# Opening stage of a gated attention and GEGLU kernel: neighbouring banks for the first units' sum pairs, three banks for the second transposes, first weights in two parts

## The chip, the core and the metric

The kernel runs on one core of a Trainium2 chip. The metric is the device time of one execution in microseconds (us). A core has a matrix engine (PE in the profile, with its weight loads as PEld), a vector engine (DVE), a scalar engine (ACT), a GpSimd engine (POOL) and a sync engine (SP), which here only issues transfers. Each engine runs its own instructions strictly in order; semaphores order them across engines. Matrix products land in eight accumulator banks, which DVE and ACT read.

## What is computed

From `reference.py`, cut to what matters:

```python
qkv = x @ wqkv                                   # 32 heads of 32
logits over 8 keys per position, 2 apart; softmax; weighted sum; @ wo     -> a
b = (gelu(x @ w_gate) * (x @ w_up)) @ w_down
g = sigmoid((x * gate_w).sum(-1, keepdims=True))
return g * a + (1 - g) * b
```

There are 2048 tokens of 1024 features; the hidden width of the second branch is 3584. All tensors are bf16.

## The kernel before

The large products are done by Winograd's form of Strassen's method on 2x2 blocks: seven block products in place of eight, paid for with sums of blocks on DVE. Tokens are handled in two halves (`s` = 0, 1) of 1024, each in two chunks of 512 columns. `c1` and `c2` hold the transposed x of the two chunks of a half; their first four and last four slices of 128 features are the blocks R11, R21 and R12, R22. T1 to T4 are sums of these blocks.

A `Unit` makes 256 outputs of one weight (two times 128) for one half of the tokens. Its products are groups of four matmuls of 128x512, each group one method call:

- `p1_` (L325 and on): L11 by R11 into bank X; ACT then copies X to bank Y (L363).
- `p2`: L12 by R21 on top of X, then ACT empties X (L347 with GELU for a gate unit, L349 for others).
- `p5`: S1 by T1 into bank V, copied out by ACT (L368).
- `p6`: S2 by T2 on top of Y; ACT copies Y to bank Z (L376).
- `p73`: S3 by T3 on top of Y, S4 by R22 on top of Z; then one DVE instruction (L387) reads Z and Y as a pair and adds the product of `p5`. Its access pattern starts at Z and steps by the distance from Z to Y (`yz`).
- `p4`: L22 by T4 on top of Y, ACT empties Y (L347 or L349), and for a gate unit applies GELU to what L387 wrote (L395).

`lie(x, v, y, z)` says which of the banks 0 to 7 a unit uses as X, V, Y, Z. Waits are set by what an instruction reads or writes, and an access that steps from one bank to another is held against everything from its first to its last byte.

The opening stage, `head()`, writes its order out by hand. It has four units: f0 and f1 (gate and up of the first pair of weight columns), f2 and f3 (gate and up of the second pair). On PE it runs in this order:

1. six warm-up matmuls (L151), then the transposes of chunk 0 (L215), emptied by DVE (L221) and ACT (L219) in turn;
2. `p1_` of f0 and f1, one small transpose (`patterns`, L260), `p2` of f0 and f1, `p1_` of f2 and f3;
3. the transposes of chunk 1, `p2` of f2 and f3, and `gate_chunk` for both chunks (L270: the mixing gate g, emptied by ACT at L273 and stored by POOL at L275);
4. `p5` of f0 to f3, `p6` of f0 to f3, `p73` of f0 to f2, `p4` of f0 to f2.

DVE meanwhile makes T1 to T4 (L1239), the sums of the first weights (`sums_pair`, L311: four steps for each pair, s0 and s1) and part of the sums of the query and key weights (`sums_qk`, L447). After `head()`, a loop over the other units runs `p1` of a unit, `p73` of the one before, `p5`, `p2` and `p6`, and `p4` of the one before; its first unit has number 2 and uses X = 0, V = 1, Y = 2, Z = 3. f3's `p73` and `p4` fall into that first round. In the gaps a planner spends a time credit per unit on DVE's background work (sums of blocks, softmax, attention products), among it `x_forms(1)` (L200), the sums for the second half of the tokens, whose x comes transposed by DMA (L328).

All weight and x loads of the opening are issued in order by SP: x of chunk 0 (two of its four tiles by ACT), the first 128 columns of the four first weight pieces (L167), x of chunk 1 (L143), the second 128 columns of these four (L167), the query and key weights (L324), 16 transposing loads (L328). A transfer counts on one of eight semaphores, taken in turn; an issue waits until the transfer eight places ahead of it has landed.

The lines that the prediction goes through are these:

```python
units[0:Q0] = f[2:]
for u, x, v, y, z in zip(f, (0, 1, 3, 5), (3, 5, 0, 1), (2, 6, 7, 4), (0, 1, 3, 5)):
    u.lie(x, v, y, z)
...
pair = _win_ap(self.Z, [[self.yz * SC, 2], [1, SC]])
```

Of the kernel before, what the change touches and what calls it, by code (L numbers as in the profile page):

```python
# [10 lines left out]
BF16 = mybir.dt.bfloat16  # L11
# [4 lines left out]
P = 128  # L16
SC = 512
# [51 lines left out]
def kernel(  # L69
# [12 lines left out]
    nc = tc.nc  # L82
# [3 lines left out]
    x = A_x.rearrange("b s d -> (b s) d")  # L86
    o2 = out.rearrange("b s d -> (b s) d")
    KT = D // P
    HK = KT // 2
# [17 lines left out]
    def reg3(kb, a, b):  # L107
        return reg(kb, a * b).rearrange("p (a b) -> p a b", a=a)

    def reg4(kb, a, b, c):  # L110
        return reg(kb, a * b * c).rearrange("p (a b c) -> p a b c", a=a, b=b)

    def regf(kb, n):
        return reg(kb, 2 * n).bitcast(F32)
# [3 lines left out]
    def bank(i):  # L118
        return banks[:, i, :]
# [17 lines left out]
    with tc.manual_schedule(engines={mybir.EngineType.PE, mybir.EngineType.DVE, mybir.EngineType.Activation,  # L137
# [9 lines left out]
        warm = reg(R_ST, SC)  # L147
        V.memset(warm, 0.0)
        for i in range(NWARM):
            pw = bank((2, 4, 6, 7)[i % 4])  # L150
            nc.tensor.matmul(pw, lhsT=warm[:, 0:P], rhs=warm, start=True, stop=True)  # L151
        wj = consts.tile([P, 1], F32, name="wj")
        nc.scalar.activation(out=wj[:], in_=warm[:, 0:1], func=ACT.Gelu_apprx_tanh)
# [5 lines left out]
        raw0 = reg4(R_W0, 2, KT, 2 * P)  # L159
# [1 line left out]
        sums0, sums1 = (reg(o, 4 * 2 * HK * P).rearrange("p (f m k n) -> p f m k n", f=4, m=2, k=HK)  # L161
                        for o in (R_WQK + 48, R_W0 + 16))

        def load_pair(dst, i, a=0, b=2 * P):
            c0 = 2 * P * i
            for m, src in ((0, B_w_gate), (1, B_w_up)):
                nc.sync.dma_start(out=dst[:, m, :, a:b], in_=src[:, c0 + a:c0 + b].rearrange("(k p) n -> p k n", p=P))  # L167

        gwr = small.tile([KT, P], BF16, tag="gwr", bufs=1)
        nc.gpsimd.dma_start(out=gwr[:], in_=gate_w.rearrange("(k p) -> k p", p=P))  # L170
        load_pair(raw0, 0, 0, P)
        load_pair(raw1, 1, 0, P)
        load_xn(1)
        load_pair(raw0, 0, P, 2 * P)
# [6 lines left out]
        for s in range(2):  # L181
            b0 = R_X[s]
            f = XF()
# [10 lines left out]
        def flat(a):  # L194
            return a.rearrange("p a b -> p (a b)")
# [8 lines left out]
            f = xf[s]  # L204
            TT(out=flat(f.T3), in0=flat(f.R22), in1=flat(f.R12), op=ALU.subtract)

        def pe_transpose_chunk(c, dst, slots, by_k):
            order = [(j, k0) for j in range(4) for k0 in range(0, KT, 4)]
            if by_k:
                order.sort(key=lambda g: g[1])  # L210
            for n_, (j, k0) in enumerate(order):
                i, o = slots[n_ % 4]
                p_ = bank(i).bitcast(BF16)[:, o * SC:(o + 1) * SC].rearrange("p (a b) -> p a b", a=4)
                for kk in range(4):
                    nc.tensor.transpose(out=p_[:, kk, :], in_=xn[c % 2][:, j, (k0 + kk) * P:(k0 + kk + 1) * P],  # L215
                                        identity=ident[:])
                d = dst[:, k0:k0 + 4, j * P:(j + 1) * P]
                if n_ % 2 == 1:
                    nc.scalar.copy(out=d, in_=p_)  # L219
                else:  # L220
                    V.tensor_copy(out=d, in_=p_)  # L221

        st_n = [0]

# [31 lines left out]
        def patterns():  # L256
            with nc.allow_low_precision("block pattern of zeros and ones"):
                V.tensor_reduce(out=R_[:], in_=ident[:].rearrange("p (h d) -> p h d", d=4), axis=AX.X, op=ALU.add)
            pgw = bank(5).bitcast(BF16)[:, 0:KT]
            nc.tensor.transpose(out=pgw, in_=gwr[:], identity=ident[0:KT, 0:KT])  # L260
            gwc = small.tile([P, KT], BF16, tag="gwc", bufs=1)
            V.tensor_copy(out=gwc[:], in_=pgw)
            V.tensor_copy(out=gwrep, in_=gwc[:].rearrange("p (k o) -> p k o", o=1).to_broadcast([P, KT, GC]))

        def gate_chunk(c, pz):
            xc = (xf[c // 2].c1, xf[c // 2].c2)[c % 2]
            for h in range(2):
                for g in range(HK):
                    kt = h * HK + g
                    nc.tensor.matmul(pz[GC * g:GC * (g + 1), :], lhsT=gwrep[:, kt, :], rhs=xc[:, kt, :],  # L270
                                     start=(h == 0), stop=(h == 1))
            z = regf(R_Z[c % 2], SC)
            nc.scalar.copy(out=z, in_=pz)  # L273
            for g in range(HK):
                nc.gpsimd.dma_start(out=z_d[g:g + 1, c * SC:(c + 1) * SC], in_=z[GC * g:GC * g + 1, :])  # L275
# [38 lines left out]
        def gu_forms(w, sm, m):  # L314
            r = lambda k0, a: (lambda kt: w[:, m, k0 + kt, a * P:(a + 1) * P])
            z = lambda n: (lambda kt: sm[:, n, m, kt, :])
            return {"L11": r(0, 0), "L12": r(HK, 0), "L22": r(HK, 1), "S1": z(0), "S2": z(1), "S3": z(2), "S4": z(3)}
# [7 lines left out]
        for c in range(2, 4):  # L325
            dst = (xf[1].c1, xf[1].c2)[c - 2]
# [91 lines left out]
        def bg(gen, prio, wake):  # L418
            t = Task(gen, prio, wake)
            tasks.append(t)  # L420
            tasks.sort(key=lambda t_: t_.prio)
            return t
# [27 lines left out]
        def qk_forms(t):  # L450
            F = {"L11": wq[0], "L12": wq[1], "S3": wq[2], "L22": wq[3], "S1": sq[0], "S2": sq[1], "S4": sq[2]}
            return {k: (lambda kt, a=a: _win_ap(a[:, kt, t:t + 1], [[NT, P]])) for k, a in F.items()}
# [3 lines left out]
        def add_unit(*a, **k):  # L456
            u = Unit(*a, **k)
            u.n = len(units)
            units.append(u)
            return u  # L460
# [18 lines left out]
        def h_task(G, U, i, s):  # L479
            h_store(G, U, i, s)  # L480
            yield 1.14 if i < NE_ else 2.35
# [7 lines left out]
        for s in range(2):  # L489
            for t in range(NT):  # L490
                u = add_unit(qk_forms(t), xf[s], "qkv", lambda s=s, t=t: qk_tile(s, t))
# [6 lines left out]
        def qk_tile(s, t):  # L498
            r = qk_raw[t % 4]
            halo = r[:, 0, SUP:SUP + HALO]  # L500
            if s == 0:
                nc.scalar.activation(out=halo, in_=ident[:, 0:HALO], func=ACT.Copy, scale=0.0)
            else:
                nc.scalar.copy(out=halo, in_=ktail[:, t, :])
            return r[:, :, 0:SUP]
# [24 lines left out]
        def v_forms(t):  # L530
            r = lambda k0, tt: (lambda kt: _win_ap(wv[:, k0 + kt, tt:tt + 1], [[NT, P]]))
            z = lambda a: (lambda kt: _win_ap(a[:, kt, 0, t:t + 1], [[4, P]]))
            return {"L11": r(0, t), "L12": r(HK, t), "S3": r(0, t + 4), "L22": r(HK, t + 4),
                    "S1": z(sv[0]), "S2": z(sv[1]), "S4": z(sv[2])}

        for s in range(2):
            for t in range(4):
                u = add_unit(v_forms(t), xf[s], "qkv", st_first if s + t == 0 else st_tile)
# [241 lines left out]
        for s in range(2):  # L780
            for t in range(NT):
                n_ = Q0 + NT * s + t
# [425 lines left out]
        n = len(units)  # L1208
# [19 lines left out]
        def head():  # L1228
            xs, f = xf[0], []
            for w, sm, o in ((raw0, sums0, R_ATTN), (raw1, sums1, R_PROD)):  # L1230
                for m in range(2):
                    u = Unit(gu_forms(w, sm, m), xs, ("gate", "up")[m], None)
                    u.T = reg3(o + 4 * m, 2, SUP)
                    f.append(u)
            units[0:Q0] = f[2:]
            for u, x, v, y, z in zip(f, (0, 1, 3, 5), (3, 5, 0, 1), (2, 6, 7, 4), (0, 1, 3, 5)):
                u.lie(x, v, y, z)
            f[3].fin = lambda: bg(h_task(f[2].T, f[3].T, 1, 0), 0, now[0] + 1)
            T = lambda o_, a, b_: TT(out=flat(o_), in0=flat(a), in1=flat(b_), op=ALU.subtract)  # L1239
            s0, s1 = sums_pair(raw0, sums0), sums_pair(raw1, sums1)  # L1240

            pe_transpose_chunk(0, xs.c1, ((0, 0), (1, 0), (3, 0), (5, 0)), False)
            f[0].p1_()
            f[1].p1_()
            patterns()
            f[0].p2()
            f[1].p2()
            f[2].p1_()
            f[3].p1_()
            pe_transpose_chunk(1, xs.c2, ((0, 0), (1, 0), (0, 1), (1, 1)), True)  # L1250
            T(xs.T1, xs.R12, xs.R11)
            next(s0)
            next(s1)
            f[2].p2()
            f[3].p2()
            for c in range(2):
                gate_chunk(c, bank(c))
            next(s0)
            T(xs.T2, xs.R22, xs.T1)
            next(s1)  # L1260
            T(xs.T3, xs.R22, xs.R12)
            for i, u in enumerate(f):
                u.p5(regf(R_XN + 2 * i, SC))
            for g in (s0, s0, s1, s1):
                next(g)
            T(xs.T4, xs.R21, xs.T2)
            for u in f:
                u.p6()
            next(sq0)
            next(sq0)  # L1270
            for u in f[:3]:
                u.p73()
            for g in (sq0, sq0, sq1, sq1):
                next(g)
            for u in f[:3]:
                u.p4()
            bg(h_task(f[0].T, f[1].T, 0, 0), 0, Q0 + 1)
# [59 lines left out]
```

## Time and profile before

| what | value |
|---|---|
| three runs | 722.19, 723.54, 723.74 us; median 723.54 |
| the profiled execution | 721.98 us, of which its span is 720.2 us |
| PE busy in the span | 709.1 us (98%) |
| DVE busy | 677.8 us (94%) |
| ACT, POOL busy | 330.9 us (46%), 134.0 us (19%) |
| TensorE clock granted | 1.00 in each stretch asked |

A row of a timeline gives start and length of a run of instructions on one engine, then the line, the operation, out<-in and how many; in brackets the idle time just before it and what ended that. A busy stretch of PE ends where the last matmul's result is out, which is later than where the next matmul could have been started: four matmuls in a row take 1.04 us from first start to last end, but follow each other at 0.216 us, so that a group of four moves the next one by 0.863 us. "x, us to landing" in a row on transfers is the time from issue until the last byte has landed.

### The profile page before, as it was taken

The numbers are of one execution on the slowest core, as the hardware profiler recorded it, in microseconds if no ns is written. First come the engines' busy times: TensorE is split into PE (matmuls) and PEld (weight loads), VectorE is DVE, ScalarE is ACT, GpSimd is POOL, SyncE is SP. The second block draws the span as 40 slices with busy tenths as digits, with TensorE's granted clock in tenths as the row PEclk, the third lists the DMA queues.
The fourth block names the chain that finished last, engine by engine and source line by source line (L and its number), as shares of the span: only waits on it lengthen the run. The fifth ranks groups of instructions, "written<-read, shape, count | busy, mean of one in ns | idle before, by whom it ended". The sixth has DMA issues, their size and how long they took to land. (4 is left out here: it accounts for less than half of the span.)

```text
span 720.2 us, 10802 instructions
## 1 busy us (share of the span) xinstructions
PE 709.1 (98%) x4099; PEld 407.1 (57%) x4099; DVE 677.8 (94%) x728; ACT 330.9 (46%) x603; POOL 134.0 (19%) x233
## 2 busy tenths in 40 slices
PE   7999999999999999999999999999999999999998
PEld 4366655655544444444444444444447886758887
DVE  3879989999999999999999999999999999899997
ACT  5454546344556665555555555555322321132431
POOL 1224543233120332131300000000200002100011
PEclk9999999999999999999999999999999999999999
DMA  9966654369263667665835836381891799995951
GB/s 245 282 150 222 190 176 143 120 235 338 92 212 118 211 231 228 197 187 182 271 111 163 282 129 190 130 310 49 283 424 64 299 404 393 420 427 227 375 232 60
DMA packets 94356, 162.04 MB, mean 225 GB/s; under 512 B 23408, under 2 KB 70928, under 8 KB 89952
## 3 DMA queue, kind: packets, MB, share of 16 engines
q1 hardware_dynamic: 77600, 105.46, 42.7%
q0 software_dynamic: 15984, 48.29, 19.3%
q10 hardware_dynamic: 720, 7.60, 2.8%
q8 instruction: 32, 0.52, 0.3%
q14 instruction: 20, 0.16, 0.1%
HBM read 112.17 MB, written 54.14 MB: 231 GB/s over the span
## 5 line engine op out<-in xcount | busy, mean ns | idle before, releaser
L341 PE MATMUL banks<-arena 128*128 128x512 bf16 x2240 | 488.0, 379 | 4.5 <-DVE arena L387 3.3
L341 PEld LDWEIGHTS <-arena 128*128 128x128 bf16 x2240 | 245.8, 110 | 244.9 <-issue 10.7
L1025 PE MATMUL banks<-arena 128*128 128x256 bf16 x1260 | 138.7, 273 | 0.6 <-DVE arena L991 0.6
L1025 PEld LDWEIGHTS <-arena 128*128 128x128 bf16 x1260 | 123.1, 98 | 16.3 <-issue 1.1
L387 DVE TENSOR_TENSOR arena<-banks,arena 128x1024 bf16<-128x1024 f32 x80 | 97.6, 1220 | 11.8 <-PE banks L341 7.8
L368 ACT COPY arena<-banks 128x512 f32<-128x512 f32 x80 | 47.0, 587 | 129.3 <-PE banks L341 129.3
L349 ACT CAST arena<-banks 128x512 bf16<-128x512 f32 x104 | 60.9, 586 | 42.8 <-PE banks L341 42.8
L726 DVE TENSOR_TENSOR arena<-arena 128x2048 bf16<-128x2048 bf16 x64 | 76.9, 1218 | 0.5
L733 DVE TENSOR_TENSOR arena<-arena 128x2048 bf16<-128x2048 bf16 (+2 forms) x96 | 73.8, 774 | 1.0
L579 DVE TENSOR_TENSOR arena<-arena 128x2048 bf16<-128x2048 bf16 x64 | 74.6, 1217 | 0.1
L1058 PE MATMUL banks<-arena 128*128 128x512 bf16 x288 | 62.8, 379 | 0.0
L248 POOL DMA_DIRECT2D h_d<-arena x28 | 20.4, 731 | 225.1 <-DVE arena L242 195.5
L376 ACT COPY banks<-banks 128x512 f32<-128x512 f32 x80 | 45.6, 570 | 23.5 <-PE banks L341 20.3
L983 DVE TENSOR_TENSOR arena<-arena 128x2304 bf16<-128x2304 bf16 x40 | 53.2, 1350 | 0.5
L363 ACT COPY banks<-banks 128x512 f32<-128x512 f32 x80 | 46.1, 576 | 14.9 <-PE banks L341 13.9
L1030 ACT COPY banks<-banks 128x256 f32<-128x256 f32 x60 | 21.4, 356 | 61.7 <-PE banks L1025 61.5
L1058 PEld LDWEIGHTS <-arena 128*128 128x128 bf16 x288 | 28.2, 98 | 33.6
L347 ACT ACTIVATE arena<-banks 128x512 bf16<-128x512 f32 x56 | 33.4, 597 | 22.7 <-PE banks L341 22.7
L906 DVE TENSOR_TENSOR arena<-arena 128x2048 bf16<-128x2048 bf16 (+1 forms) x40 | 41.8, 1109 | 0.2 <-DMA arena<-h_d 0.2
L311 DVE TENSOR_TENSOR arena<-arena 128x1024 bf16<-128x1024 bf16 x64 | 41.1, 685 | 0.5
L991 DVE TENSOR_TENSOR arena<-arena 128x2304 bf16<-128x2304 bf16 x28 | 37.6, 1349 | 0.2
L242 DVE TENSOR_TENSOR arena<-arena 128x2048 bf16<-128x2048 bf16 x28 | 33.9, 1214 | 0.5 <-ACT arena L349 0.5
(88 smaller groups left out, 410.7 us busy)
## 6 DMA issues: line engine op xcount, KB each, us to landing
arena<-t_d SPq DMA_DIRECT2D x8, 2304.0 KB, 14.7
h_d<-arena POOLq DMA_DIRECT2D x28, 512.0 KB, 4.7
arena<-w_c SPq DMA_DIRECT2D x12, 1152.0 KB, 14.3
t_d<-arena POOLq DMA_DIRECT2D x36, 256.0 KB, 3.9
arena<-h_d SPq DMA_DIRECT2D x6, 1536.0 KB, 12.6
arena<-in_B_w_down_dram SPq DMA_DIRECT2D x28, 256.0 KB, 7.0
arena<-in_B_w_gate_dram SPq DMA_DIRECT2D x14, 512.0 KB, 5.5
arena<-in_B_w_up_dram SPq DMA_DIRECT2D x14, 512.0 KB, 4.7
```

Of the source, the lines that this page charges most:

```text
L341: self.pe = nc.tensor.matmul(ps, lhsT=self.L[form](kt), rhs=rhs[:, kt, :], start=(start and kt == 0), stop=(kt == HK - 1), skip_group_chec ...
L349: nc.scalar.copy(out=o_, in_=i_)
L363: nc.scalar.copy(out=self.Y, in_=self.X)
L368: nc.scalar.copy(out=self.p5s, in_=self.V)
L376: nc.scalar.copy(out=self.Z, in_=self.Y)
L387: TT(out=self.T[:, :, c2s], in0=pair, in1=self.p5s.rearrange("p (o n) -> p o n", o=1).to_broadcast([P, 2, SC]), op=ALU.add)
L579: TT(out=dst, in0=q.rearrange("p (o s) -> p o s", o=1).to_broadcast([P, NWIN, AC]), in1=_win_ap(k, [[-DIL, NWIN], [1, AC]]), op=ALU.mult)
L726: TT(out=prod2[(t // 2) % 2][:, t % 2], in0=ab, in1=_win_ap(v[:, t, HALO:HALO + AC], [[SJ, NJ], [-DIL, NWIN], [1, SJ]]), op=ALU.mult)
L733: TT(out=out_, in0=h(0), in1=h(1), op=ALU.add)
L983: TT(out=o_, in0=a, in1=b_, op=op)
L1025: nc.tensor.matmul(c(i, h, j), lhsT=l[:, kt, j * P:(j + 1) * P], rhs=r[:, kt, :], start=False, stop=(kt == KH - 1), skip_group_check=True)
L1058: nc.tensor.matmul(ps, lhsT=L[:, i, j * P:(j + 1) * P], rhs=R[:, i, :], start=(start and q == 0), stop=(q == NK - 1), skip_group_check=not ...
```

## The change

Four edits, all in the opening stage:

- The banks of the four units: each unit's Y and Z are now neighbours, with Z one above Y.
- The transposes of chunk 1 go through three whole banks in turn in place of four halves of two banks; their order, four groups of the first feature half and then four of the second, stays. `p2` of f2 comes ahead of them. The first step of s0 is placed on DVE after the fifth of the eight copies (`then`), where it came after T1 before.
- The first weights (gate and up of the first pair, first 128 columns) are loaded in two parts each: k slices 0 to 3 of gate, then of up, then 4 to 7 of gate, then of up. That makes two more transfers on SP's queue.
- Three small uses of banks move with this (warm-up, `patterns`, `gate_chunk`).

```diff
-            pw = bank((2, 4, 6, 7)[i % 4])
+            pw = bank((2, 4, 6, 0)[i % 4])
...
-        def load_pair(dst, i, a=0, b=2 * P):
+        def load_pair(dst, i, a=0, b=2 * P, k0=0, k1=KT):
             c0 = 2 * P * i
             for m, src in ((0, B_w_gate), (1, B_w_up)):
-                nc.sync.dma_start(out=dst[:, m, :, a:b], in_=src[:, c0 + a:c0 + b].rearrange("(k p) n -> p k n", p=P))
+                nc.sync.dma_start(out=dst[:, m, k0:k1, a:b],
+                                  in_=src[k0 * P:k1 * P, c0 + a:c0 + b].rearrange("(k p) n -> p k n", p=P))
...
-        load_pair(raw0, 0, 0, P)
+        load_pair(raw0, 0, 0, P, 0, HK)
+        load_pair(raw0, 0, 0, P, HK, KT)
         load_pair(raw1, 1, 0, P)
...
-        def pe_transpose_chunk(c, dst, slots, by_k):
+        def pe_transpose_chunk(c, dst, slots, by_k=False, then={}):
...
-                i, o = slots[n_ % 4]
-                p_ = bank(i).bitcast(BF16)[:, o * SC:(o + 1) * SC].rearrange("p (a b) -> p a b", a=4)
+                p_ = bank(slots[n_ % len(slots)]).bitcast(BF16)[:, 0:SC].rearrange("p (a b) -> p a b", a=4)
...
+                if n_ in then:
+                    then[n_]()
...
-            pgw = bank(5).bitcast(BF16)[:, 0:KT]
+            pgw = bank(7).bitcast(BF16)[:, 0:KT]
...
-            for u, x, v, y, z in zip(f, (0, 1, 3, 5), (3, 5, 0, 1), (2, 6, 7, 4), (0, 1, 3, 5)):
+            for u, x, v, y, z in zip(f, (3, 5, 1, 7), (1, 7, 3, 5), (2, 0, 4, 6), (3, 1, 5, 7)):
...
-            pe_transpose_chunk(0, xs.c1, ((0, 0), (1, 0), (3, 0), (5, 0)), False)
+            pe_transpose_chunk(0, xs.c1, (3, 5, 1, 7))
...
             f[3].p1_()
-            pe_transpose_chunk(1, xs.c2, ((0, 0), (1, 0), (0, 1), (1, 1)), True)
+            f[2].p2()
+            pe_transpose_chunk(1, xs.c2, (3, 5, 1), True, {4: lambda: next(s0)})
             T(xs.T1, xs.R12, xs.R11)
-            next(s0)
             next(s1)
-            f[2].p2()
             f[3].p2()
             for c in range(2):
-                gate_chunk(c, bank(c))
+                gate_chunk(c, bank(3 + 2 * c))
```

## The prediction

> **What bounds the kernel now.** I read the page's busy table first:
>
> ```profile
> span 720.2 us, 10802 instructions
> PE 709.1 (98%) x4099; PEld 407.1 (57%) x4099; DVE 677.8 (94%) x728; ACT 330.9 (46%) x603; POOL 134.0 (19%) x233
> ```
>
> PE bounds the whole, with 709.1 of 720.2 us, so it can gain only where it waits. Then PE's waits (total, times, longest), of which this is the largest:
>
> ```profile
> PE banks L341 <- DVE arena L387: 3.3, 6, 1.1
> ```
>
> Then PE's timeline, which says where:
>
> ```profile
> 7.20 1.04 PE L341 MATMUL banks<-arena 128*128 128x512 bf16 x4 [0.29 <-DVE arena L221]
> 8.76 1.04 PE L341 MATMUL banks<-arena 128*128 128x512 bf16 x4 [0.52 <-DMA arena<-in_B_w_up_dram]
> ...
> 9.83 3.63 PE L341 MATMUL banks<-arena 128*128 128x512 bf16 x16
> 13.30 0.61 PE L215 MATMUL banks<-ident,arena 128*128 128x128 bf16 x8
> ...
> 16.74 0.38 PE L215 MATMUL banks<-ident,arena 128*128 128x128 bf16 x4 [0.28 <-ACT arena L219]
> 16.96 1.89 PE L341 MATMUL banks<-arena 128*128 128x512 bf16 x8
> 18.78 1.05 PE L270 MATMUL banks<-arena 128*32 128x512 bf16 x16
> 19.75 9.67 PE L341 MATMUL banks<-arena 128*128 128x512 bf16 x44
> ...
> 29.95 1.89 PE L341 MATMUL banks<-arena 128*128 128x512 bf16 x8 [0.52 <-DVE arena L387]
> 32.36 1.89 PE L341 MATMUL banks<-arena 128*128 128x512 bf16 x8 [0.52 <-DVE arena L387]
> 34.69 29.51 PE L341 MATMUL banks<-arena 128*128 128x512 bf16 x136 [0.45 <-DVE arena L387]
> ```
>
> From 34.69 on PE runs 136 matmuls without a gap. 16 take 3.63 us and 136 take 29.51, so one moves the next by 25.88 / 120 = 0.2157, and a group of four by 0.863; 0.17 more passes until its last result is out (1.04). What the change saves or loses before 34.69 moves everything behind it, unless something there doesn't move along.
>
> **The change part by part.**
>
> *First weights in two parts.* At 8.76 f1's `p1_` comes late, waiting for all of up; f0's came at 7.20, held by a copy, with all of gate there. Now f1 needs only half of up, behind half of gate: as many bytes as all of gate, so it is there by about 7.2. f1 starts at 7.20 + 0.863 = 8.06, 0.70 earlier. The 16 matmuls behind it shift along (ACT empties banks between them at the old distance) and hand over at 12.48.
>
> *`p2` of f2 ahead of the transposes, three banks.* From 13.30 to 16.96 PE spends 3.66 us on eight groups of four transposes, though a group moves the next by 0.22 (0.61 for two, less the tail): half of it is waiting for two banks to be emptied. Copies take, on ACT and DVE:
>
> ```profile
> 13.98 0.59 ACT L219 COPY arena<-banks 128x512 bf16<-128x512 bf16 x1
> 16.49 0.42 DVE L221 COPY arena<-banks 128x512 bf16<-128x512 bf16 x1 [0.47 <-PE banks L215]
> ```
>
> In the new order f2's `p2` runs 12.48 to 13.34 and its last result is out at 13.51. ACT empties it, bank 1, until 14.14 (0.60, in a row below). Groups 0 and 1 start at 13.34 and 13.56; group 2 goes to bank 1: 14.19, 0.4 of wait. Group 3 (bank 3, emptied at 14.2) follows at 14.41, group 4 (bank 5, emptied by ACT at 14.65) at 14.69, and its copy on DVE ends at 15.55. Groups 5, 6 and 7 each find a bank emptied just ahead of them: 15.09, 15.47, 15.70. f3's `p2` runs 15.92 to 16.78, and PE would be at L270 at 16.9 in place of 18.78.
>
> *It doesn't keep that.* The first sum (L311) now stands on DVE between the copies of groups 4 and 6, and it reads the second halves of the first weights. The last of them, by the timeline of SP and its landing in the view of transfers:
>
> ```profile
> 9.95 0.58 SPq L167 DMA_DIRECT2D arena<-in_B_w_up_dram  x1
> ...
> arena<-in_B_w_up_dram SPq DMA_DIRECT2D x1, 256.0 KB, 6.5
> ```
>
> It lands at 9.95 + 6.5 = 16.4. DVE's timeline:
>
> ```profile
> 16.83 1.22 DVE L1239 TENSOR_TENSOR arena<-arena 128x2048 bf16<-128x2048 bf16 x1
> 17.96 1.89 DVE L311 TENSOR_TENSOR arena<-arena 128x1024 bf16<-128x1024 bf16 x3
> ...
> 26.19 2.35 DVE L447 TENSOR_TENSOR arena<-arena 128x2048 bf16<-128x2048 bf16 x2
> 28.67 1.23 DVE L387 TENSOR_TENSOR arena<-banks,arena 128x1024 bf16<-128x1024 f32 x1
> 31.08 1.23 DVE L387 TENSOR_TENSOR arena<-banks,arena 128x1024 bf16<-128x1024 f32 x1 [1.18 <-PE banks L341]
> 33.42 1.23 DVE L387 TENSOR_TENSOR arena<-banks,arena 128x1024 bf16<-128x1024 f32 x1 [1.11 <-PE banks L341]
> 34.56 4.62 DVE L447 TENSOR_TENSOR arena<-arena 128x2048 bf16<-128x2048 bf16 x4
> ```
>
> DVE stands from 15.55 to 16.47. L311 steps by 0.60 (three in 1.89), so group 6's copy runs 17.08 to 17.50 and T1 17.42 to 18.63. L270 writes that group's bank: 17.55, a wait of 0.7. It is through at 18.6, and `p5`, which needs T1, starts at 18.68 against 19.75: **1.07** is kept of 1.9. DVE itself gains nothing: T1 is 0.59 later with one L311 (0.60) less behind it, so the last L447 ends where it did, at 28.53, and f0's L387 starts at 28.45.
>
> *Neighbouring banks.* At 29.95, 32.36 and 34.69 PE waits for the L387 of another unit. f1's S4 product goes to bank 1, which L387 of f0 steps over between 0 and 2; f2's bank 3 lies between 1 and 6; f1's Y, 6, between 3 and 7. With neighbours no such case is left. In steps of PE: 19.75 + 44 x 0.2157 = 29.24 against 29.95 is 0.71; 29.95 + 1.73 = 31.68 against 32.36 is 0.68; 32.36 + 1.73 = 34.09 against 34.69 is 0.60: **1.99**. `p4` must still follow its own unit's L387. From 18.68 without a gap it starts at 18.68 + 14 x 0.863 = 30.76 for f0 and 32.49 for f2; the L387 of f0 is done at 29.68, of f2 (products out at 30.93) at 32.2. The gaps of 1.18 and 1.11 close on DVE: its four L447 run 32.1 to 36.7, just when f3's products are out.
>
> *A new wait.* f1's Y is now bank 0, and unit 2's first product goes there right behind f2's `p4`, at 33.36. ACT must have emptied it:
>
> ```profile
> 34.28 0.60 ACT L347 ACTIVATE arena<-banks 128x512 bf16<-128x512 f32 x1 [6.84 <-PE banks L341]
> 34.77 1.05 ACT L395 ACTIVATE arena<-arena 128x1024 bf16<-128x1024 bf16 x1
> 35.75 0.59 ACT L349 CAST arena<-banks 128x512 bf16<-128x512 f32 x1
> ```
>
> From the start of f0's L347, past its GELU, to the end of f1's L349 is 2.06. f0's `p4` is out at 30.76 + 1.04 = 31.80, so bank 0 is free at 33.90 and PE goes on at 33.95: **0.59** lost. Behind it on ACT stand f2's L347 and GELU and unit 2's copy, out at about 36.0; PE wants that copy's bank at 33.95 + 4 x 0.863 = 37.4.
>
> *Work that isn't earlier.* SP's queue paces the transposing loads, so they stay, and L200 needs all of them:
>
> ```profile
> L328 SPq DMA_TRANSPOSE arena<-in_A_x_dram x16: 1258/1259/5895, 18.3 to 45.3; - x16
> DMA to landing us min/median/max: 2.5/2.8/12.5
> ...
> 48.73 2.48 DVE L200 TENSOR_TENSOR arena<-arena 128x2048 bf16<-128x2048 bf16 x2
> 51.37 1.23 DVE L387 TENSOR_TENSOR arena<-banks,arena 128x1024 bf16<-128x1024 f32 x1 [0.16 <-PE banks L341]
> ```
>
> The last lands at 45.3 + 2.8 = 48.1. The second L200, at 49.87 now, would be at 47.4, so it waits 0.7; L387 behind it starts at 49.3 in place of 48.9. PE wants the bank three groups (2.6) after the products and L387 takes 1.23: 0.9 is still spare, so nothing is lost here. Past that, each microsecond costs one.
>
> *The two added transfers.* Two more issues on SP, at most 0.58 each by the row above. Bounds: the second halves later by all of it, 1.2, or, if smaller parts flow better, 0.3 earlier. I take nothing, since an issue behind them stood blocked for most of its time, where a free one takes 0.6, and bytes stay the same:
>
> ```profile
> 2.80 2.93 SPq L167 DMA_DIRECT2D arena<-in_B_w_gate_dram  x1
> ```
>
> The Trainium skill (DMA: Bandwidth & Descriptors, Anatomy of one DMA — SWDGE (gpsimd) path) speaks against the split: each transfer costs about 2.0 us plus its bytes over 436 GB/s, fitted on the software path. Paid in series, that is by estimate from this page 4.0 us for two more, and the kernel would end 1.5 us slower; the same section puts most of the 2 us into the completion, which needn't be in series. No row here prices a transfer alone.
>
> *The sum.* 1.07 + 1.99 - 0.59 = 2.47 us. The profiled execution took 721.98 (its span of 720.2 and 1.8 around it), so 719.5. It lay 1.6 under the median of the three runs, 723.54, against which I forecast **721.1 us**.
>
> **The rivals.**
>
> 1. *Later second halves.* Each microsecond past 16.4 costs one. With the issue time of 1.2 the gain is 1.3: 722.3. For it: SP's queue has no rest until 45.3. Against: the blocked issue of 2.93.
> 2. *Slower: a fixed price for each transfer, in series on the queue ahead of the second halves.* From 1.24 us each (2.47 / 2) the gain is gone. As an upper bound by rows stands the shortest landing, 2.5: twice that is 5.0, so 723.54 - 2.47 + 5.0 = 726.1. Against it: eight transfers of 256 KB lie between the landings of up's first half (8.7, ending the wait at 8.76) and second (16.4), 0.96 each; at the highest rate of a slice on the page, 427 GB/s, 256 KB take 0.61, which leaves at most 0.35 as a fixed price.
>
> ```profile
> GB/s 245 282 150 222 190 176 143 120 235 338 92 212 118 211 231 228 197 187 182 271 111 163 282 129 190 130 310 49 283 424 64 299 404 393 420 427 227 375 232 60
> ```
>
> 3. *The split pairs were not what held PE.* Then it still waits for L387, which is only 0.22 earlier (28.45 for 28.67): 723.3, no change. Against: the three waits end 0.05 after an L387 whose two banks none of the waiting products touches.
> 4. *The transposing loads late as well.* If all are issued 1.2 later, L200 waits until 49.3, and L387 ends some 0.4 too late: 721.5.
> 5. *More is kept.* Second halves 0.3 earlier and ACT soon enough to halve the new wait: 720.5.
>
> **How the numbers follow.** Chances: forecast 0.58, rival 1 0.14, rival 2 0.07, rival 3 0.06, rival 4 0.07, rival 5 0.08. The forecast's own range is 0.3 either way for the landing and the spread of the runs around their median (722.19 to 723.74): 719.4 to 721.6. To leave out no more than 2 in 10 I go up past rivals 1 and 4: 719.3 to 722.7. A measurement of this kernel tells about 0.2%, 1.45 us, from nothing. Faster: the forecast but for its edge, rivals 4 and 5, a little of 1: 0.73. Same: rival 3, most of 1, that edge: 0.20. Slower: rival 2: 0.07.
>
> **What would show it.** Right: f0's and f1's `p1_` as one run of eight from 7.2; a wait of PE of half a microsecond for DVE L221 ahead of L270 at 17.5; L311 between two L221 on DVE, near 16.5, after a wait for a load; `p5` at 18.7; no wait for L387 before 60 us; one of about 0.4 (the tail hides 0.17) for ACT L349 near 34; the second L200 after a wait for x. Unit 2's first product then comes at 33.95, against 34.69 + 8 x 0.2157 = 36.42. Wrong: L311 well after 16.5, waits for L387 that stay, or waits of PE behind 60 us that grow and give the opening's gain back.

## The result, and the profile after

The changed kernel takes 720.44 us in the median of 5 runs (719.86 to 721.05) against 723.54 for the kernel before (5 runs, 722.15 to 723.86): a ratio of 0.9969, with a 95% interval of 0.9957 to 0.998. The forecast was 721.1. Run once more on another chip, the same file took 720.39 (5 runs, 719.92 to 720.82) against 722.49, a ratio of 0.9966 [0.9954, 0.9978].

The two profiled executions differ by less, 1.2 us of span (719.0 against 720.2). The head of the page after:

```profile
span 719.0 us, 10759 instructions
PE 705.6 (98%) x4043; PEld 407.6 (57%) x4099; DVE 677.4 (94%) x728; ACT 330.6 (46%) x603; POOL 134.4 (19%) x233
```

(56 matmul records are missing there, 4043 for 4099, so some counts below are one or two short.) The change moves the lines of kernel.py by one to three: L390 is L387 of before, L352 is L349, L314 is L311, L222 is L221, L202 is L200. PE's timeline after, opening; columns as before: start, time, line, what, and in brackets PE's idle time just before and what ended it:

```profile
4.37 2.46 PE L216 MATMUL banks<-ident,arena 128*128 128x128 bf16 x32 [0.43 <-DMA arena<-in_A_x_dram]
7.12 1.89 PE L344 MATMUL banks<-arena 128*128 128x512 bf16 x8 [0.29 <-DVE arena L222]
...
17.46 1.05 PE L273 MATMUL banks<-arena 128*32 128x512 bf16 x16 [0.49 <-DVE arena L222]
18.59 14.84 PE L344 MATMUL banks<-arena 128*128 128x512 bf16 x67
```

The eight `p1_` products run as one from 7.12 (forecast 7.2), the wait of half a microsecond for L222 stands at 17.46 (17.55), and `p5` starts at 18.59 (18.68). The same view further on:

```profile
33.80 17.43 PE L344 MATMUL banks<-arena 128*128 128x512 bf16 x78 [0.38 <-ACT arena L352]
52.10 10.52 PE L344 MATMUL banks<-arena 128*128 128x512 bf16 x47 [0.87 <-DVE arena L390]
62.55 1.48 PE L587 MATMUL banks<-arena,ones_r 128*32 128x512 bf16 x24
...
121.40 4.48 PE L344 MATMUL banks<-arena 128*128 128x512 bf16 x20 [1.11 <-DVE arena L390]
...
664.18 51.44 PE L1028 MATMUL banks<-arena 128*128 128x256 bf16 x468 [0.61 <-DVE arena L994]
```

and of the kernel before, the rows that answer to the last three:

```profile
64.14 1.48 PE L584 MATMUL banks<-arena,ones_r 128*32 128x512 bf16 x24
122.98 4.48 PE L341 MATMUL banks<-arena 128*128 128x512 bf16 x20 [1.11 <-DVE arena L387]
...
665.75 51.43 PE L1025 MATMUL banks<-arena 128*128 128x256 bf16 x468 [0.61 <-DVE arena L991]
```

Unit 2's first product starts at 33.80 in place of 36.42, so the opening won 2.62 us; no wait for L390 is left in it. But at 62.55 the lead is 64.14 - 62.55 = 1.59, and from there it stays: 1.58 at 121.40, 1.57 at 664.18. (Another 0.4 goes behind VectorE's last step, at the very end of the span; its cause isn't shown.) About 1.0 of the 2.62 is lost in one place, the wait of 0.87 at 52.10: without it PE would have gone on at 33.80 + 80 x 0.2157 = 51.06. VectorE shows what PE waited for:

```profile
16.38 0.69 DVE L314 TENSOR_TENSOR arena<-arena 128x1024 bf16<-128x1024 bf16 x1 [0.77 <-DMA arena<-in_B_w_up_dram]
16.99 0.42 DVE L222 COPY arena<-banks 128x512 bf16<-128x512 bf16 x1
17.32 1.22 DVE L1242 TENSOR_TENSOR arena<-arena 128x2048 bf16<-128x2048 bf16 x1
...
46.12 1.22 DVE L202 TENSOR_TENSOR arena<-arena 128x2048 bf16<-128x2048 bf16 x1
49.69 1.23 DVE L202 TENSOR_TENSOR arena<-arena 128x2048 bf16<-128x2048 bf16 x1 [2.36 <-DMA arena<-in_A_x_dram]
50.84 1.22 DVE L390 TENSOR_TENSOR arena<-banks,arena 128x1024 bf16<-128x1024 f32 x1
```

The second L202 (L200 before) stood 2.36 us for x, until 49.69, and L390, which PE needs, is queued behind it. Was the load issued later? No: the view of its line gives 45.3 for the last issue, as before.

```profile
L331 SPq DMA_TRANSPOSE arena<-in_A_x_dram x16: 1258/1260/5667, 18.7 to 45.3; - x16
```

It landed later. The view of transfers, cut to the moment of that one issue, has the median time from issue to landing at the end of the row; first the kernel before, then after:

```profile
arena<-in_A_x_dram SPq DMA_TRANSPOSE x1, 2.8
```

```profile
arena<-in_A_x_dram SPq DMA_TRANSPOSE x1, 3.9
```

2.8 against 3.9 us. What else had moved is on POOL, the kernel before first, then after:

```profile
46.84 0.58 POOL L510 DMA_DIRECT2D q_d<-arena  x1 [22.64 <-DVE arena L387]
```

```profile
44.23 0.58 POOL L513 DMA_DIRECT2D q_d<-arena  x1 [21.33 <-DVE arena L390]
44.80 0.55 POOL L514 DMA_DIRECT2D k_d<-arena  x1
45.40 0.77 POOL L289 DMA_DIRECT2D zc<-z_d  x1
46.16 1.50 POOL L251 DMA_DIRECT2D h_d<-arena  x2
```

These are unit 2's stores, the gate's small load and the first products' stores. They start 2.6 us earlier, as PE came earlier, and now fall among the last transposing loads.

### The profile page after: what moved, and what is told of

The parts are those of the page before. It is cut to its first block, busy times and chain, and to the rows that moved or that the text cites. A ratio compares the mean times of both kernels' runs of the same rounds, so it can differ in the third digit from the quotient of the medians.

```text
span 719.0 us, 10759 instructions
## 1 busy us (share of the span) xinstructions
PE 705.6 (98%) x4043; PEld 407.6 (57%) x4099; DVE 677.4 (94%) x728; ACT 330.6 (46%) x603; POOL 134.4 (19%) x233
## 5 line engine op out<-in xcount | busy, mean ns | idle before, releaser
L1028 PEld LDWEIGHTS <-arena 128*128 128x128 bf16 x1260 | 123.1, 98 | 16.4 <-issue 1.1
L390 DVE TENSOR_TENSOR arena<-banks,arena 128x1024 bf16<-128x1024 f32 x80 | 97.5, 1220 | 9.2 <-PE banks L344 5.0
L352 ACT CAST arena<-banks 128x512 bf16<-128x512 f32 x104 | 60.9, 585 | 43.0 <-PE banks L344 43.0
L582 DVE TENSOR_TENSOR arena<-arena 128x2048 bf16<-128x2048 bf16 x64 | 74.6, 1217 | 0.1
L314 DVE TENSOR_TENSOR arena<-arena 128x1024 bf16<-128x1024 bf16 x64 | 41.2, 685 | 1.4 <-DMA arena<-in_B_w_up_dram 1.0
```

Source lines behind the costliest of these rows:

```text
L352: nc.scalar.copy(out=o_, in_=i_)
L390: TT(out=self.T[:, :, c2s], in0=pair, in1=self.p5s.rearrange("p (o n) -> p o n", o=1).to_broadcast([P, 2, SC]), op=ALU.add)
L582: TT(out=dst, in0=q.rearrange("p (o s) -> p o s", o=1).to_broadcast([P, NWIN, AC]), in1=_win_ap(k, [[-DIL, NWIN], [1, AC]]), op=ALU.mult)
L1028: nc.tensor.matmul(c(i, h, j), lhsT=l[:, kt, j * P:(j + 1) * P], rhs=r[:, kt, :], start=False, stop=(kt == KH - 1), skip_group_check=True)
```

## The experiments

My theory: the opening's chain is won as forecast, and what is lost at 52 us comes from the later landing of x. Rivals: the split loads, the place of L314, or the stores did it; or the loss is only moved by any cure. The diffs are against the changed kernel. Times are medians of the runs named; "before" is the kernel before on the same chip, 722.31 (30 runs) for the first four.

**Neighbouring banks undone for the four units.**

```diff
-(3, 5, 1, 7), (1, 7, 3, 5), (2, 0, 4, 6), (3, 1, 5, 7)
+(3, 5, 1, 7), (1, 7, 3, 5), (0, 6, 2, 4), (3, 1, 5, 7)
```

> The changed kernel with its four Y banks dealt out anew (0, 6, 2, 4 in place of 2, 0, 4, 6), so that f0's pair steps over bank 1 and f1's over bank 5, the banks of the next unit's S4 product; Z, X and V stay. Theory (an access that steps over a bank makes PE wait for it): two waits of PE for L390 come back. p5 starts at 18.6 as before, f1's S4 would be ready at 28.1 and waits for f0's L390 (28.34 + 1.23) until 29.6; f2's S4 waits for f1's until 32.0; the wait for L352 at 33.8 is gone, since bank 0 is now f0's Y. Unit 2's first product at 35.4 in place of 33.80; of these 1.6 us about 1 is given back where the second L202 waits for the transposing loads, so the time is some 0.6 over the changed kernel's 720.4. Rival (the pairs weren't what held PE): no wait for L390 near 30, unit 2's first product at 33.3.

723.04 us (10 runs, 721.97 to 725.13), ratio 1.0011 [1.0, 1.0022]. PE's timeline of this run:

```profile
30.86 1.02 PE L344 MATMUL banks<-arena 128*128 128x512 bf16 x4 [1.21 <-DVE arena L390]
33.27 32.10 PE L344 MATMUL banks<-arena 128*128 128x512 bf16 x148 [1.39 <-DVE arena L390]
```

The waits for L390 are back, 2.6 us in these two rows, and the wait for L352 and the one at 52 us are gone. That a product waits for a step whose two banks merely enclose its own is thereby shown. In the times the whole gain is gone, 2.6 us where 0.6 was expected. The profile shows two things. The first thing is that f2 is held at its S3 product and not only at S4, as was expected. In steps of PE the two waits are 2.9 (from 29.48 to 30.86 and from 31.72 to 33.27). The second is that `p5` began 1.40 late in this execution (19.99 for 18.59, the first transposes took 3.60 us), which nothing took up. The row of 62.55 stands at 65.31, 2.76 later: 1.40 and 2.9, less the 0.55 for L352 (0.38 and the tail of 0.17) and the 1.04 at 52 us that are gone. By this estimate the banks alone cost some 1.3 us. How much of the median's 2.6 is theirs isn't shown: the ten runs spread over 3.2 us, three of them at a mean granted clock of 0.997. On the landing this run says nothing, since POOL began at 48.01 and the load took 2.5 us.

**First weights in one part again.**

```diff
-        load_pair(raw0, 0, 0, P, 0, HK)
-        load_pair(raw0, 0, 0, P, HK, KT)
+        load_pair(raw0, 0, 0, P)
```

> The changed kernel with the first weights in one part again. Theory (L314 between the copies sets the pace, and it waits for the second halves of the weights whatever PE does): f1's first product at 8.7 in place of 7.98, but L314 still at 16.4 within 0.2, L273 after a smaller wait, p5 at 18.6 to 18.8, unit 2's first product at 33.8 to 34.0; time as the changed kernel's within 0.3. Rival (each part's saving adds up): p5 and all behind it 0.7 later, unit 2 at 34.5. If the two transfers fewer bring SP's queue forward, the second halves land earlier than 16.29 and L314 starts before 16.3.

720.4 us (9 runs), ratio 0.9971 [0.9961, 0.9981]: no difference in the time, as expected. What the split does in the opening isn't shown by the profile, since this opening was late for another reason; from PE's timeline:

```profile
4.61 3.59 PE L215 MATMUL banks<-ident,arena 128*128 128x128 bf16 x32 [0.67 <-DMA arena<-in_A_x_dram]
...
34.72 7.50 PE L343 MATMUL banks<-arena 128*128 128x512 bf16 x34 [0.38 <-ACT arena L351]
```

The first 32 transposes took 3.59 us in place of 2.46, and unit 2 started 0.92 later than in the changed kernel. Yet the row that stands at 62.55 there stands at 62.49 here: PE did not wait at 52 us. Nearly a microsecond lost in the opening cost nothing, although the load landed as late as there (its L201 starts at 49.63, for 49.69).

**The products' stores late.** They go out behind unit 3's stores.

```diff
-            nc.gpsimd.dma_start(out=h_d[s][e][:, :, i0 // 2, :], in_=...)
+            def put():
+                nc.gpsimd.dma_start(out=h_d[s][e][:, :, i0 // 2, :], in_=...)
+            at(Q0 + 3, put) if i < 2 and s == 0 else put()
```

> The changed kernel with the two stores of the first hidden pair (POOL, 512 KB each, issued at 46.1 and 46.8) put behind the next unit's stores, at about 53. Theory (POOL's stores moved forward with PE and now share the DMA engines with the last transposing loads): the last of these lands near 48.3 in place of 49.2, the second L202 starts near 48.4 in place of 49.69, PE's wait of 0.87 at 52.1 is gone, everything behind is 1.0 earlier and the time 719.4. The q_d, k_d and zc transfers from 44.2 on stay, so a part of the lateness may stay too. Rivals: SP issues the loads too late (then 49.2 and 49.69 stay), or the landing varies by itself from run to run (then it may be anything, with no tie to the stores).

722.55 us (10 runs), ratio 1.0006 [0.9996, 1.0016]. That theory falls: the load still landed 3.8 us after its issue, and the second L202 waited until 49.39. What is new is a cost: the stores hold a buffer that the products of unit 2 need. VectorE of this run (L588 is L582 of the changed kernel):

```profile
49.39 1.23 DVE L202 TENSOR_TENSOR arena<-arena 128x2048 bf16<-128x2048 bf16 x1 [2.13 <-DMA arena<-in_A_x_dram]
...
62.34 2.36 DVE L588 TENSOR_TENSOR arena<-arena 128x2048 bf16<-128x2048 bf16 x2 [3.52 <-DMA h_d<-arena]
```

**The differences of the second token half a unit later**, so that nothing on VectorE waits for x at 48 us.

```diff
-        due(Q0 + NT, bg(late_forms(), 3, Q0 + 1))
+        due(Q0 + NT, bg(late_forms(), 3, Q0 + 2))
```

> The changed kernel with the sums for the second half of the tokens (L202) let in one unit later, by which the planner also orders the background work behind them anew. Theory (the second L202, in order on DVE ahead of a unit's L390, is where PE loses 0.87): no wait of DVE for the transposing loads, no wait of PE near 52, everything from 60 us on about 1.0 earlier, time 719.4. Rival (the loss only moves, because DVE has as much to do): a wait of PE for L390 of about the same size between 52 and 120, time 720.4.

723.29 us (10 runs, 721.5 to 724.75), ratio 1.0007 [0.9994, 1.002]. The wait at 52 us is gone, and a larger one stands later in place of the 1.11:

```profile
33.77 27.79 PE L344 MATMUL banks<-arena 128*128 128x512 bf16 x128 [0.38 <-ACT arena L352]
...
122.40 3.83 PE L344 MATMUL banks<-arena 128*128 128x512 bf16 x17 [3.18 <-DVE arena L390]
```

The rival was right that the loss only moves, and it grows: 1.06 is won by 62 us and 2.07 lost at 122. VectorE has no room for the moved work between 55 and 120 us. The median lies above the profiled execution's 721.8: six of the ten runs, 723.25 to 724.75, had a mean granted clock of 0.995 to 0.998, the four at 1.0 took 721.5 to 722.9.

The next four ran beside a "before" of 722.1 us (23 runs).

**Nothing on POOL while x lands.** As the late stores, and besides:

```diff
-            nc.gpsimd.dma_start(out=q_d[s][:, t, :], ...)
-            nc.gpsimd.dma_start(out=k_d[s][:, t, :], ...)
+            at(Q0 + 3, put) if s + t == 0 else put()
...
-        bg(gate_task(0), 0, 0)
+        bg(gate_task(0), 0, Q0 + 1)
```

(`put` issues the two stores.)

> All stores and the gate's load that POOL issues between 44 and 48 us (unit 2's q_d and k_d, zc, and the products' h_d) are put behind the next unit's stores, at about 50 us or later; only their place changes. Read here is the landing of the last transposing load of x and the second step L202, not the total: the products' late stores hold their buffer and will cost some us after 62 us, as in the run with late stores (722.55 us). Theory: the small POOL transfers among the transposing loads are what delays the last landing (3.86 us after its issue in the changed kernel, 2.77 us in the kernel before): with POOL quiet it lands in 2.5 to 2.8 us, at 47.9 to 48.2 us, L202 starts at once, and PE's wait for L390 at about 52 us is gone. Rival: the landing does not depend on POOL's transfers: it still takes 3.4 to 3.9 us, L202 starts after 49 us, and PE waits 0.4 to 1 us at 52 us.

The view of transfers at the last issue, 45.4 again, then VectorE:

```profile
arena<-in_A_x_dram SPq DMA_TRANSPOSE x1, 2.7
```

```profile
48.64 1.23 DVE L202 TENSOR_TENSOR arena<-arena 128x2048 bf16<-128x2048 bf16 x1 [1.72 <-DMA arena<-in_A_x_dram]
```

2.7 us in place of 3.9; L202 starts 1.05 earlier, and PE's wait at 52 us fell to 0.23. The theory holds for the landing, in this one execution. L202 did not start "at once": 48.64 is 0.5 after the landing at 45.4 + 2.7, as 49.69 is in the changed kernel after 45.3 + 3.9. Over the fourteen profiles of this study the same load took 2.5 to 2.8 us in the four where POOL began at 46.8 or later, and 3.2 to 5.0 us in the ten where it began at 43.9 to 45.1. That is what ties the late landing to POOL's transfers. With the products' stores taken away alone it stayed late, so the small ones ahead of them (q_d, k_d, zc) are enough for it; no run parts these from each other, or keeps the large ones without them. The Trainium skill (DMA: Bandwidth & Descriptors, Issuing engines are not separate DMA queues) says that transfers issued from any engine run on the same 16 DMA engines and interleave; the later landing beside POOL's transfers fits that.

The single run of this kernel, 723.56, carries the late stores' cost in the first two rows of PE's timeline, and in the third something further, told at the end:

```profile
63.57 0.40 PE L599 MATMUL banks<-arena,ones_r 128*32 128x512 bf16 x4 [1.02 <-DVE arena L594]
64.71 0.40 PE L599 MATMUL banks<-arena,ones_r 128*32 128x512 bf16 x4 [0.74 <-DVE arena L594]
65.04 13.99 PE L350 MATMUL banks<-arena 128*128 128x512 bf16 x56
```

**Two more gains in the opening.** L314 behind T1 again, and unit 2's X to bank 5, so that its first product needn't wait for L352.

```diff
-            pe_transpose_chunk(1, xs.c2, (3, 5, 1), True, {4: lambda: next(s0)})
+            pe_transpose_chunk(1, xs.c2, (3, 5, 1), True)
             T(xs.T1, xs.R12, xs.R11)
+            next(s0)
...
-                self.lie((0, 5)[n % 2] if two[0] else 0, 1, (2, 4)[n % 2], 3)
+                self.lie((0, 5)[n % 2] if two[0] else 5 * (n == Q0), 1, (2, 4)[n % 2], 3)
```

> Two more gains in the opening, from taking work off its chain: the first step L314 goes behind T1 on VectorE as before, so PE should not wait for T1 (about 0.5 us), and unit 2's first sum goes to bank 5, so its first product does not wait for f2's L352 (0.4 us). Theory: what the opening wins beyond about 1.6 us is given back at 52 us, where the second L202 waits for the last landing of x, whatever PE did before: unit 2's first product comes 0.6 to 1.1 us earlier (at 32.7 to 33.2 us), PE's wait for L390 at 52 us grows by as much to 1.5 to 2 us, and the time stays within 0.4 us of the changed kernel's 720.4. Rival: the opening still sets the time, and the whole 0.6 to 1.1 us arrives at the end: 719.4 to 719.9 us.

721.21 us (11 runs, 720.66 to 724.02), ratio 0.9992 [0.9982, 1.0001]: rather slower than the change, by more than the 0.4 allowed. PE, then VectorE:

```profile
18.88 32.12 PE L344 MATMUL banks<-arena 128*128 128x512 bf16 x148 [0.26 <-DVE arena L314]
52.80 10.52 PE L344 MATMUL banks<-arena 128*128 128x512 bf16 x48 [1.80 <-DVE arena L390]
```

```profile
50.39 1.22 DVE L202 TENSOR_TENSOR arena<-arena 128x2048 bf16<-128x2048 bf16 x1 [3.29 <-DMA arena<-in_A_x_dram]
```

PE now runs from 18.88 past unit 2 without a wait, and pays 1.80 at 52.80. Unit 2 starts at 18.88 + 68 x 0.2157 = 33.55, only 0.25 earlier, where 0.6 to 1.1 was expected: `p5` now waits for L314 behind T1, and the first transposes were slow again (3.24 us). The load was issued at 45.8, took 4.5 us and landed 1.1 later than in the changed kernel; L202 and PE's row at 52 us are 0.70 later. So PE goes on when the landing lets it, whatever the opening won, which is the theory's direction. That the earlier opening made the landing later is likely, as POOL began at 43.99, but one execution doesn't show it.

**The same, and the first unit's products may start one unit earlier.**

```diff
-                due(n_ + 4, bg(qk_prods(units[n_], s, t), 2, n_ + 2))
+                due(n_ + 4, bg(qk_prods(units[n_], s, t), 2, n_ + (1 if n_ == Q0 else 2)))
```

> As the run with both opening gains, and the first unit's products with L581 may begin one unit earlier, so that VectorE does them while the last part of x lands and L390 does not stand behind the second L202. Theory (the second L202 was the limit, because L390 was queued behind it): PE's wait at 52 us falls from 0.9 to 0.4 us or less, and the two opening gains now count: 0.8 to 1.4 us less than the changed kernel, 719.0 to 719.6 us. Rival: the delay is only moved on, as it was when the second token half's differences were begun a unit later (there 0.9 us gone at 52 us came back as 2.1 us more at 122 us): the wait at 122 us grows by what was won and the time is 720.2 us or more.

719.75 us (5 runs, 719.05 to 719.8), ratio 0.9959 [0.9946, 0.9971]. VectorE (the expectation's L581 is L582 here), then PE:

```profile
46.35 3.50 DVE L582 TENSOR_TENSOR arena<-arena 128x2048 bf16<-128x2048 bf16 x3 [0.51 <-ACT arena L352]
49.77 1.22 DVE L390 TENSOR_TENSOR arena<-banks,arena 128x1024 bf16<-128x1024 f32 x1
...
51.02 3.73 DVE L202 TENSOR_TENSOR arena<-arena 128x2048 bf16<-128x2048 bf16 x3
```

```profile
51.04 10.52 PE L344 MATMUL banks<-arena 128*128 128x512 bf16 x48 [0.16 <-DVE arena L390]
61.49 1.48 PE L587 MATMUL banks<-arena,ones_r 128*32 128x512 bf16 x24
...
120.34 4.48 PE L344 MATMUL banks<-arena 128*128 128x512 bf16 x20 [1.13 <-DVE arena L390]
```

VectorE works through the time in which it stood, L390 comes ahead of the L202 that needs x, and the load, 4.5 us on its way here too, keeps nobody. The wait near 120 us did not grow (1.13 against 1.11), so the rival falls. PE's row of 62.55 stands at 61.49: 1.06 earlier, the span 1.0 shorter. The median lies 0.7 under the changed kernel's 720.44, a little less than the 0.8 to 1.4 expected.

**Eight warm-up products.** `NWARM = 6` becomes 8.

> The changed kernel with 8 instead of 6 warm-up products, so that PE has work until x lands at about 4.4 us, or even a little beyond (each takes about 0.43 us). Theory: the slow first transposes of some runs (32 in 3.6 us where others take 2.46 us) come from the idle 0.4 to 1 us after the warm-up products; with it filled the transposes run 2.5 us in the profile, whatever x does, and the spread of the runs (719.86 to 721.05) falls below 0.7 us. Rival: the clock doubles at a moment that is not tied to the idle time; then weight loads 0.107 us apart still show in the transposes of some runs, the spread stays about 1.2 us, and where x lands at 4.4 us the two products cost up to 0.4 us at the start, most of which the wait at 52 us takes up.

721.54 us (12 runs, 719.7 to 723.52), ratio 0.9988 [0.9977, 1.0]. The theory falls, and so does the rival's spread of 1.2. The profiled transposes ran at full pace from 4.36, but the spread grew to 3.8 us. Three runs, 723.25 to 723.52, had a mean granted clock of 0.998; what lowered it there isn't known.

The last three with times ran beside a "before" of 722.49 (13 runs). **The changed kernel again, unaltered:**

> The changed kernel once more, unaltered, beside the two below on one chip: it says how far its start and its last landing of x differ from execution to execution. Theory: the moment at which TensorE's clock goes up (weight loads of the transposes 0.056 us apart in place of 0.107) and the landing of the last transposing load (2.5 to 5.0 us after its issue so far) both differ by execution, and the second L202 takes up what the first one costs: 719.7 to 722.5 us over the runs, median 720.4 to 721.2. Rival: the kernel's time is as settled as the kernel's before (30 runs within 1.5 us but for four): all runs within 719.8 to 721.1.

720.39 us (5 runs, 719.92 to 720.82): as settled as the rival said. Its profile, PE's timeline:

```profile
4.89 3.60 PE L216 MATMUL banks<-ident,arena 128*128 128x128 bf16 x32 [0.94 <-DMA arena<-in_A_x_dram]
...
34.56 27.79 PE L344 MATMUL banks<-arena 128*128 128x512 bf16 x128 [0.38 <-ACT arena L352]
62.28 1.48 PE L587 MATMUL banks<-arena,ones_r 128*32 128x512 bf16 x24
```

The opening again ran late, by 0.76 at unit 2 (34.56 against 33.80), and was taken up: the 128 products from 34.56 on run past 52 us without a wait, and the row of 62.55 stands at 62.28. The load landed earlier here too (3.2 us after its issue, POOL having begun at 44.98).

**Only the products earlier** (the last edit above, alone), and **these and bank 5, without moving L314:**

> The changed kernel, with one edit: the first unit's products L581 may begin one unit earlier. VectorE then does them while the last part of x lands, and L390 comes ahead of the second L202. Theory: this alone ends the dependence on the landing, so PE's wait at 52 us falls from 0.9 to 0.4 us or less, the opening's whole gain is kept, and unit 2's start at 33.8 us carries through: 719.3 to 720.2 us, with a smaller spread than the unaltered changed kernel. Rival: the gain of the run with three edits (719.75 us) came from the opening's two; then this one stays at 720.4 us or more.

719.99 us (7 runs, 719.57 to 721.59), ratio 0.9967 [0.9956, 0.9978]. PE's wait at 52 us is 0.16, so the cure works alone, and the row of 62.55 stands at 61.92. By times it can't be told from the changed kernel beside it, and the spread, 2.0 us, is not the smaller one expected but over twice that kernel's 0.9.

> As the run with three edits (719.75 us), but the first step L314 stays between the transposes' copies as the change has it. Theory: L314 ahead of T1 costs PE about 0.5 us of wait for T1, as the changed kernel's DVE rows show (a stand of 0.77 us for the load, then the copy and T1 behind it), so this comes out 0.3 to 0.6 us slower than with L314 behind T1: 719.4 to 720.3 us. Rival: L314's place is nothing or a gain, since one step less stands behind T1: 719.0 to 719.4 us.

719.56 us (6 runs, 719.14 to 722.25), ratio 0.996 [0.9947, 0.9974], as with L314 moved. Whether L314's place costs anything stays open: the eight `p1_` products of this opening began 1.2 late, and so late the load that L314 needs is there.

**The kernel before again**, one execution:

> The kernel before once more, unaltered, for one more profile of its start. In its first profile TensorE's clock was up when the first transposes began (32 of them, weight loads 0.056 us apart); in most later profiles of the other kernels it went up some microseconds later. Theory: where it goes up late, the kernel before loses the whole of it, since VectorE has no wait for x at its second L200: the row of L584 at 64.14 us comes later by as much as the first transposes end late, and the span grows by the same, 0.5 to 2 us. Rival: a later step takes it up here too, and L584 stays at 64.1 us, the span at 720.2. If the clock is up early again (before 5 us), this run says nothing on it.

Inconclusive. The opening was late by only 0.24 at the 136 matmuls (34.93 against 34.69); L584 came 0.49 later, and the span was 721.3. Nothing was taken up, but the lateness was small. The run with the banks apart says more: it has no wait for x at 52 us either, and its late start of 1.40 arrived at 65.31 in full.

## Why the prediction was right

*First weights in two parts:* right in the profile, since the eight products run as one from 7.12; that the split was needed is not shown, as the one run without it had a late opening.

*Transposes and L314:* right. L314 stands between two L222, at 16.38 after 0.77 of waiting for up's second half, T1 at 17.32, and `p5` started within 0.1 of the forecast. This rests on the rows alone: no run undoes `p2`'s place and the three banks by themselves.

*The added transfers:* right at nothing. Up's last part let L314 start at 16.38, where 16.4 was worked out. Rivals 1 and 2 fall with this row; the Trainium skill's fixed 2.0 us for each transfer (DMA: Bandwidth & Descriptors, Anatomy of one DMA — SWDGE (gpsimd) path; fitted on the software path), paid in series, is not what this queue shows.

*Neighbouring banks and the new wait:* right. With the banks apart the waits return; the new wait is 0.38 for L352, as forecast. Rivals 3 and 5 fall. Unit 2 came 2.62 earlier, for a sum of 2.47.

*The step that failed:* "The last lands at 45.3 + 2.8 = 48.1" and "0.9 is still spare, so nothing is lost here". The landing was taken from the trace of before as if it were a property of the load. It depends on what else is in flight, and the change itself brought POOL's transfers forward by 2.6 us into it. The second L202 started at 49.69, 1.6 after 48.1: 1.1 is the longer landing, 0.5 the time from landing to start, which the prediction put at nothing. L390 behind it started at 50.84 in place of 49.3, 1.54 later. PE lost 1.04 of that, so the spare was 0.5 and not 0.9. "No wait for L387 before 60 us", one of the signs of being right, was therefore not met. Rival 4 had the place, but at 0.4 us and by the wrong cause: nothing was issued later.

*Why the time came out all the same:* the profiles' gain is 1.2, half of the sum, while the medians on that chip differ by 3.1. The runs of before there lie at 722.15, 722.19 and at 723.54 to 723.86, and its median falls in the upper group. In the three later sets of runs the median of before is 722.1 to 722.5, and where the change ran beside it the medians differ by 2.1. From 722.3 the same sum would have given 719.8, against 720.4. So it was in part luck that 721.1 was met: one term was lost, and an offset between profile and median that I had carried over unexamined made up for it. Why the medians differ by more than the profiles is argued, not shown: the changed kernel, with a wait in reserve at 52 us, takes up a late start, as its repeat and the run with the first weights in one part do, and the kernel before has no such wait.

## What to carry to other kernels

When PE is brought forward, list every transfer that its results release, and see which loads those will now meet; a landing time read from the trace of before holds only for the traffic of before. A wait that remains caps every gain ahead of it: with the second L202 still in the way, two more gains in the opening brought nothing, while putting the steps of VectorE in another order (work that is ready first, the step that needs the late load last) removed the wait. The two best versions here do that and take 719.75 and 719.56 us, 0.9959 and 0.9960 of before. Against the change at 0.9969 and 0.9966 their lead is seen in the profiles, but the intervals overlap.

## What the hardware showed beside this

*The clock at the start.* Identical first transposes took 2.46 us in the changed kernel's profile and 3.60 in its repeat. The weight loads of TensorE show the difference; the kernel before first, then the repeat:

```profile
4.42 0.90 PEld L215 LDWEIGHTS <-arena 128*128 128x128 bf16 x16 [1.39 <-DMA arena<-in_A_x_dram]
```

```profile
4.88 3.33 PEld L216 LDWEIGHTS <-arena 128*128 128x128 bf16 x32 [1.85 <-DMA arena<-in_A_x_dram]
```

16 in 0.90 us are 0.056 each, 32 in 3.33 are 0.104: about half the pace. The moment of change differs by execution with the same code. That it is the clock is inferred from the pace alone, since the granted clock in the view of windows reads 1.00 from the start of the span in both profiles. The Trainium skill (TensorE: Matmul & The Clock Gate, What's actually happening) states that the clock is halved until a free-running window of 3.4 us was busy; the pace, and a moment of change that isn't tied to the code, agree.

*The clock later.* In the run with POOL quiet, PE waited for products near 64 us. The view of windows, columns: stretch, length, busy time (instructions) of PE, weight loads, VectorE, ScalarE, POOL, then granted clock, DMA share, GB/s:

```profile
62.10:65.50 3.40, 1.64 (x22) 0.66 (x11) 3.15 (x11) 0.10 (x1) 0.00 (x0) 1.00 0.01 2
65.50:68.90 3.40, 3.40 (x9) 1.31 (x8) 3.40 (x6) 1.14 (x2) 1.73 (x4) 0.50 0.11 37
68.90:72.30 3.40, 3.40 (x17) 2.27 (x16) 3.33 (x5) 1.39 (x5) 1.19 (x3) 1.00 0.25 86
```

After 3.4 us in which PE was busy for 1.64, though never idle for longer than about 1 us, the clock was 0.50 for the next 3.4 us. That cost another 1.7 us: the 56 products from 65.04 on took 13.99 us, where the 56 from 80.81 on take 12.31. The same section of the Trainium skill puts the fall after an idle window; here a window half busy was enough. It doesn't follow each time: in the profile of the differences a unit later, PE stood for 3.18 us ahead of 122.40 and the clock stayed at 1.00. One such dip makes 1.7 / 720 = 0.24% of a mean clock, which is the 0.998 of the slower runs with eight warm-up products; that those, or the slower runs of the differences a unit later, had a dip too is not shown.
